# Output projections of token chunks 0-2 as products of 512 columns, the last 128 output columns computed transposed

## The chip, the cores and the metric

One core of a Trainium2 chip runs the whole kernel. The metric is the device time of one execution in microseconds (us). "Span" is the length of the profiled execution, about 2 us shorter than the time.

Engines: PE is TensorE, PEld its weight loads, DVE is VectorE, ACT is ScalarE; SPq and ACTq are the DMA issues on the SyncE and ScalarE queues. A "product" is one matmul instruction: PEld loads its stationary 128 x 128 operand (a weight load), and the columns of the other operand move past it. A "spread" is a DMA that copies 1/den to the partitions where DVE needs it; a "scaling" is the DVE pass that multiplies a part of phi(q) by it; the "scaled operand" PQ is what comes out.

## The reference, cut to what matters

```python
# x: 2048 tokens x 640; both branches read layernorm(x)
xn = _layernorm(x, axis=-1)
return x + _A_ref(xn, A_wqkv, A_wo) + _B_ref(xn, B_w1, B_b1, B_w2, B_b2)
# A: linear attention, 32 heads of 20, phi(q) (phi(k)^T v) / den, then @ wo
# B: gelu(xn @ w1 + b1) @ w2 + b2, 1536 hidden
```

The kernel folds attention's inner product and `wo` into a 640 x 640 matrix M. The output of a token is then 12 blocks of gelu(h) times W2 plus 5 blocks of the scaled phi(q) times M, plus x, plus b2: 17 products of 128 x 128 by 640 columns for each tile of 128 tokens. There are 16 tiles, in four chunks of four.

## The kernel before: the parts that matter

```python
# scaling phi(q) by 1/den, one chunk, on DVE: three passes, each behind its own "spread" DMA
def scale_pq(c): ...
    for r, (lo, n) in enumerate(((0, 2), (2, 2), (4, 1))):
        tensor_tensor(out=PQ[:, lo:lo+n, cc], in0=PQ[:, lo:lo+n, cc],
                      in1=rsp[:, c, r:r+1, :].broadcast_to(...), op=mult)
def spread(c): ...        # three DMAs on ACT's queue: rden -> rsp[:, c, r, :]
def x_again(c): ...       # reload of x, on the sync queue
# [... cut ...]
HALF = [(0, HW), (HW, D)]                 # HW = 320, D = 640: two PSUM banks a tile
out_mm(0, 0, JT, b0, HALF[:1], [b0])      # half of tile 0's first 12 products
den_mm(b0 + 1)                            # denominators
m_step(...)                               # M
den_rec()                                 # reciprocal on DVE
for c in range(NC): spread(c)
scale_pq(0)
# ... the first 12 products of tiles 3, 0, 1, 2 without the scaled operand ...
for t, b in enumerate(ahead):             # then their 5 products with it
    xb(t)                                 # x + b2 on DVE
    out_mm(t, JT, NS, b, HALF, [b, b + 1])
    out_done(t, b)                        # PSUM + (x + b2) on DVE, DMA out on the sync queue
for t in range(4, NT - 1):
    ...; out_mm(t, 0, NS, b, HALF, [b, b + 1]); out_done(t, b)
# [... last tile in three pieces ...]
```

Each of the 17 products of a tile is issued as two of 320 columns, with the same stationary operand loaded twice.

## Time and profile before

| | before |
|---|---|
| time, median of six runs | 207.47 us (207.40 to 207.63) |
| span | 205.6 us |
| products / weight loads recorded | 1539 / 1539 |
| PEld busy share | 66% |
| start of first output product to start of last DVE addition | 126.32 to 203.39: 77.07 us |

From the page of the kernel before: span, busy times and shares, then the chain of work that ended last, by engine.

```profile
span 205.6 us, 3863 instructions
...
PE 202.2 (98%) x1539; PEld 135.2 (66%) x1539; DVE 109.6 (53%) x227; ACT 71.4 (35%) x133; POOL 35.1 (17%) x85
...
PE 96%; DVE 1%; DMA 1%; issue 0%; ACT 0%; DVEq 0%
```

PE is the engine that bounds it. The timeline of PE in the kernel before (start, duration, engine, line, operation, operands, shape, count):

```profile
126.32 1.79 PE L671 MATMUL ps<-W,HG 128*128 128x320 bf16 x12
128.04 1.26 PE L618 MATMUL ps<-PQ,ZB 128*32 128x512 bf16 x20
129.13 1.80 PE L608 MATMUL ps<-Wo,W 128*32 128x320 bf16 x48
130.87 11.58 PE L671 MATMUL ps<-W,HG 128*128 128x320 bf16 x84
142.29 5.60 PE L671 MATMUL ps<-Msb,PQ 128*128 128x320 bf16 x40
...
152.34 3.42 PE L671 MATMUL ps<-W,HG 128*128 128x320 bf16 x24
...
156.96 3.42 PE L671 MATMUL ps<-W,HG 128*128 128x320 bf16 x24
```

Read starts, not durations: in this trace products overlap (24 of them have a duration of 3.42 us and a turn of 24 x 0.1358 = 3.26 us). A tile takes 156.96 - 152.34 = 4.62 us for 34 products, 135.8 ns each. The line at 142.29 is where PE first needs the scaled operand PQ; it follows without a gap.

The hand-over in the kernel before: the reload of x on the sync queue, the reciprocal, the twelve spreads, and the scalings of chunk 0 with what they waited for.

```profile
126.76 2.38 SPq L247 DMA_DIRECT2D xnT<-in_A_x_dram  x4
...
132.25 3.34 DVE L628 RECIPROCAL rden<-den_sb 128x512 bf16<-128x512 f32 x1
135.62 9.81 ACTq L247 DMA_DIRECT2D xn_tm<-rden  x12
138.83 0.69 DVE L633 TENSOR_TENSOR PQ<-PQ,xn_tm 128x1024 bf16<-128x1024 bf16 x1 [3.25 <-DMA xn_tm<-rden]
139.79 1.03 DVE L633 TENSOR_TENSOR PQ<-PQ,xn_tm 128x1024 bf16<-128x1024 bf16 x2 [0.27 <-DMA xn_tm<-rden]
```

The last scaling ends at 140.8. PE wants the first scaled block at 142.29, so there is room.

### The profile page before, as it was taken

To read this page: it belongs to the slowest core of one execution; us is meant where nothing else is said; L and a number is where in the kernel's file an instruction comes from. 1 tells how busy PE (TensorE), PEld (TensorE's weight loads), DVE (VectorE), ACT (ScalarE), POOL (GpSimd) and SP (SyncE) were. 2 spreads that over 40 slices of the span, in tenths; PEclk is the share of its full clock that TensorE was granted. 3 is DMA by queue.
4 is the path that set the end of the run, shared out by engine and by line. 5 is a ranking of instruction groups with operands and counts; after the bars stand their busy time and mean duration, and the time that the engine had idled before them with its cause. 6 is when DMAs were issued, how large, how long until landed. Compare 5 with 4: busy or idle time off the path is not lost.

```text
span 205.6 us, 3863 instructions
## 1 busy us (share of the span) xinstructions
PE 202.2 (98%) x1539; PEld 135.2 (66%) x1539; DVE 109.6 (53%) x227; ACT 71.4 (35%) x133; POOL 35.1 (17%) x85
## 2 busy tenths in 40 slices
PE   8999999999999999999999999999999999999995
PEld 3898767544457777777746445677777777777774
DVE  3784388100007888999358888734764322523322
ACT  2787777666676455111153554300000000000000
POOL 3342156800000001999000200000000000000000
PEclk9999999999999999999999999999999999999999
DMA  5967846699920000000000000968611100100111
GB/s 153 351 169 122 204 127 123 81 360 327 368 90 0 0 0 3 0 0 3 0 0 3 2 0 19 364 182 171 152 64 63 35 32 32 37 32 32 35 37 59
DMA packets 24842, 19.69 MB, mean 96 GB/s; under 512 B 9976, under 2 KB 24824, under 8 KB 24824
## 3 DMA queue, kind: packets, MB, share of 16 engines
q1 hardware_dynamic: 23072, 17.86, 29.5%
q10 hardware_dynamic: 1752, 1.58, 4.1%
q8 instruction: 12, 0.20, 0.4%
q14 instruction: 6, 0.05, 0.1%
HBM read 13.11 MB, written 2.62 MB: 77 GB/s over the span
## 4 chain that ended last, share of the span: by engine, by line
PE 96%; DVE 1%; DMA 1%; issue 0%; ACT 0%; DVEq 0%
PE ps L671 36%; PE ps L380 26%; PE ps L513 11%; PE ps L488 11%; PE ps L554 10%; DMA xPK<-in_A_x_dram 1%; DVE stats L331 1%; PE ps L608 1%; PE ps L564 1%; PE ps L618 1%; PE ps L318 0%; DVE xn_tm L353 0%; DVE W L722 0%; PE ps L361 0%; PE ps L537 0%
## 5 line engine op out<-in xcount | busy, mean ns | idle before, releaser
L671 PE MATMUL ps<-W,HG 128*128 128x320 bf16 (+2 forms) x396 | 54.8, 295 | 0.0
L380 PE MATMUL ps<-xnT,W 128*128 128x128 bf16 (+3 forms) x405 | 52.7, 292 | 0.1
L671 PEld LDWEIGHTS ps<-W,HG 128*128 128x128 bf16 x396 | 38.1, 98 | 14.5 <-ACT Msb L590 0.2
L380 PEld LDWEIGHTS ps<-xnT,W 128*128 128x128 bf16 x405 | 33.8, 98 | 18.4 <-DMA W<-in_B_w_dram 0.4
L384 ACT ACTIVATE HG<-ps,b1c 128x128 bf16<-128x128 f32 (+3 forms) x81 | 39.1, 515 | 14.4 <-PE ps L380 13.3
L682 DVE TENSOR_TENSOR W<-ps,xnT 128x640 bf16<-128x640 f32 x15 | 12.4, 825 | 35.8 <-PE ps L671 34.6
L476 ACT ACTIVATE ek<-ps 128x512 bf16<-128x512 f32 (+1 forms) x36 | 23.2, 645 | 20.4 <-PE ps L554 10.7
L477 DVE TENSOR_SCALAR ek<-ek 128x512 bf16<-128x512 bf16 (+1 forms) x36 | 11.0, 305 | 32.4 <-ACT ek L476 31.2
L671 PE MATMUL ps<-Msb,PQ 128*128 128x320 bf16 (+2 forms) x165 | 24.2, 295 | 0.0
L554 PE MATMUL ps<-xnT,Wqkv 128*128 128x512 bf16 x100 | 21.9, 379 | 0.0
L513 PE MATMUL ps<-xPK,xn_tm 128*128 128x320 bf16 x160 | 21.9, 299 | 0.0
L488 PE MATMUL ps<-Wqkv,xnT 128*128 128x320 bf16 x160 | 21.9, 299 | 0.0
L671 PEld LDWEIGHTS ps<-Msb,PQ 128*128 128x128 bf16 x165 | 15.9, 98 | 5.9
L488 PEld LDWEIGHTS ps<-Wqkv,xnT 128*128 128x128 bf16 x160 | 15.7, 98 | 6.2
L513 PEld LDWEIGHTS ps<-xPK,xn_tm 128*128 128x128 bf16 x160 | 15.7, 98 | 6.1
L507 POOL COPY Wqkv<-Wqkv 128x128 bf16<-128x128 bf16 x25 | 15.1, 603 | 22.9 <-PE ps L488 21.4
L331 DVE BATCH_NORM_STATS2 stats<-xPK 128x6 f32<-128x320 bf16 x32 | 14.0, 477 | 9.3 <-DMA xPK<-in_A_x_dram 9.2
L554 PEld LDWEIGHTS ps<-xnT,Wqkv 128*128 128x128 bf16 x100 | 9.7, 98 | 11.4
L479 DVE SCALAR_TENSOR_TENSOR PQ<-ps,ek 128x512 bf16<-128x512 f32 x20 | 13.8, 692 | 2.1
L479 DVE SCALAR_TENSOR_TENSOR xPK<-ps,ek 128x640 bf16<-128x640 f32 x16 | 13.2, 825 | 1.7
L525 DVE TENSOR_TENSOR Msb<-Msb,xPK 128x640 f32<-128x640 f32 x14 | 11.6, 825 | 0.5
L341 POOL TENSOR_TENSOR rstd<-aggr,mhalf 128x1 f32<-128x1 f32 x16 | 9.9, 620 | 8.9 <-DVE aggr L339 8.9
(57 smaller groups left out, 77.4 us busy)
## 6 DMA issues: line engine op xcount, KB each, us to landing
xnT<-in_A_x_dram SPq DMA_DIRECT2D x4, 640.0 KB, 6.8
Wqkv<-in_A_wqkv_dram SPq DMA_DIRECT2D x3, 800.0 KB, 6.8
out_dram<-W SPq DMA_DIRECT2D x15, 160.0 KB, 1.8
W<-in_B_w_dram SPq DMA_DIRECT2D x4, 480.0 KB, 6.1
W<-in_B_w_dram SPq DMA_DIRECT2D x1, 1920.0 KB, 13.0
xn_tm<-rden ACTq DMA_DIRECT2D x12, 128.0 KB, 3.4
xPK<-in_A_x_dram SPq DMA_DIRECT2D x4, 320.0 KB, 5.5
Wo<-in_A_wo_dram SPq DMA_DIRECT2D x8, 160.0 KB, 8.4
```

Of the source, the lines that this page charges most:

```text
L331: Pl.ins(v, lambda e: e.bn_stats(stats[:, s, 6 * h:6 * h + 6], x_in[:, t, h * HW:(h + 1) * HW]), reads=r_x[t], writes=[r_stats[s][h]])
L380: Pl.ins(pe, [(lambda e, k=k: e.matmul(bank(b, 0, w), W1[:, k, jb * P:(jb + 1) * P], xnT[:, k, tok], start=(k == 0), stop=(k == DT - 1))) ...
L384: Pl.ins(s_, lambda e: e.activation(HG[:, jb, tok], bank(b, 0, w), ACT.Gelu_apprx_tanh, bias=b1c[:, jb:jb + 1]), reads=[B_[b], r_b1c], wri ...
L476: Pl.ins(s_, lambda e: e.activation(e2, src, ACT.Exp), reads=br, writes=[r_ek[s]])
L479: Pl.ins(v, lambda e: e.scalar_tensor_tensor(out=d2, in0=src, scalar=0.0, in1=e2, op0=ALU.max, op1=ALU.add), reads=br + [r_ek[s]], writes= ...
L488: fns.append(lambda e, k=k, h=h, b=b, t=t: e.matmul(bank(b + h, 0, HW), xnT[:, k, t * P:(t + 1) * P], Wqkv[:, k, D + h * HW:D + (h + 1) * ...
L507: Pl.ins(g, lambda e, k=k, i=i: e.tensor_copy(plain(Wqkv[:, k, D:2 * D], i), parts(Wqkv[:, k, 0:D], i)), reads=[r_Wq], writes=[r_Wk, r_WqP])
L513: Pl.ins(pe, [(lambda e, t=t, h=h, b=b, f=f, i=i: e.matmul(bank(b + h, 0, HW), xn_tm[:, t, f * P:(f + 1) * P], PK[:, t, h * HW:(h + 1) * H ...
L525: Pl.ins(v, lambda e, t=t: e.tensor_tensor(out=zsum, in0=zsum, in1=PK[:, t, :], op=ALU.add), reads=[r_PK[t], r_zsum], writes=[r_zsum])
L554: Pl.ins(pe, [(lambda e, k=k, j=j, b=b: e.matmul(bank(b), Wqkv[:, k, D + j * P:D + (j + 1) * P], xnT[:, k, cc], start=(k == 0), stop=(k == ...
L671: Pl.ins(pe, [(lambda e, i=i, x=x, bb=bb: e.matmul(bank(bb, 0, x[1] - x[0]), seq[i][0], seq[i][1][:, x[0]:x[1]], start=(i == 0), stop=(i = ...
L682: Pl.ins(v, lambda e: e.tensor_tensor(out=halves(out_sb[:, s, :]), in0=pair(b), in1=halves(x_res[:, t, :]), op=ALU.add), reads=B_[b:b + 2] ...
```

## The change

Its intent is that all output products of chunks 0 to 2 have 512 columns, one full bank. Columns 0-511 go tile by tile: 17 products of 512 columns instead of 34 of 320. Columns 512-639 of a whole chunk are computed transposed: the 128 weight columns are stationary, the chunk's 512 tokens move, so another 17 products of 512. That result is transposed back by DMA before it is stored, and the matching part of x has to be transposed too before it can be added.

```diff
+        # x's last 128 columns: load in rows of 256 bytes, then transpose, on the sync queue
+        dma("sync", xrem..., xv[0:(NT - CH) * P, MW:D]..., [r_xrem] + r_PK)
+        for c in range(NC - 1):
+            dma_t("sync", xrT[:, c * CW:(c + 1) * CW]..., xrem[:, c * CW:(c + 1) * CW], [r_xrT[c]], reads=[r_xrem])
+        def rem_mm(c, lo, hi, b):       # stationary W2 / M columns 512-639, 512 tokens move
+        def rem_done(c, b):             # + b2 + xrT on DVE, dma_t back, DMA out (sync queue)
+        def main_done(t, b):            # 512 columns; DMA out now on ACT's queue
...
-        out_mm(0, 0, JT, b0, HALF[:1], [b0])
-        den_mm(b0 + 1)
+        out_mm(0, 0, JT, MAIN, first[:1])        # MAIN = [(0, 512)]
+        den_mm(bb[1])
...
-        for t, b in enumerate(ahead):
+        for t in range(1, CH):
+            out_mm(t, 0, JT, MAIN, first[t:t + 1])
+        rem_mm(0, 0, JT, first[CH])
+        for t in range(CH):
             xb(t)
-            out_mm(t, JT, NS, b, HALF, [b, b + 1])
-            out_done(t, b)
+            out_mm(t, JT, NS, MAIN, first[t:t + 1])
+            main_done(t, first[t])
...                                      # chunks 1, 2 alike; chunk 3 stays in halves
```

More of the change, by code (lines that the diff above doesn't have):

```diff
@@ L127, in bass_parallel_sum__linear_attn_block__dense_activation_gelu__prompt_kernel @@
     HH = H // 2
+    MW = D - P
     TA, TB = P // HH, P // H
@@ L183, in bass_parallel_sum__linear_attn_block__dense_activation_gelu__prompt_kernel @@
         out_sb = W1f[:, 2 * DT * D:2 * DT * D + 2 * D].rearrange("p (s d) -> p s d", s=2)
+        xPf = xPK[:].rearrange("p t d -> p (t d)")
+        xrT = xPf[:, 0:(NC - 1) * CW]
+        remT = xPf[:, (NC - 1) * CW:NC * CW]
+        remO = xPf[:, NC * CW:(NC + 1) * CW].rearrange("p (t d) -> p t d", t=CH)
+        xrem = xPf[:, (NC + 1) * CW:2 * NC * CW]
+        b2t = sb("b2t", [P, 1], BF16)
+        b2c = sb("b2c", [P, 1], FP32)
         ps = es.enter_context(nc.psum_tensor("ps", [P, 8 * 512], FP32))
@@ L234, in bass_parallel_sum__linear_attn_block__dense_activation_gelu__prompt_kernel @@
         r_out = [R_("out0"), R_("out1")]
+        r_xrT = [R_("xrT%d" % c) for c in range(NC - 1)]
+        r_xrem, r_remT, r_remO, r_b2t, r_b2c = R_("xrem"), R_("remT"), R_("remO"), R_("b2t"), R_("b2c")
         xv = A_x.rearrange("b s d -> (b s) d")
@@ L461, in bass_parallel_sum__linear_attn_block__dense_activation_gelu__prompt_kernel @@
             .rearrange("p a d -> p (a d)"), [r_b2])
+        dma("sync", b2t[:], B_b2[MW:D].rearrange("(p a) -> p a", a=1), [r_b2t])
         for w in range(NW):
@@ L646, in x_again @@
         def x_again(c):
-            dma("sync", x_res[:, c * CH:(c + 1) * CH, :],
-                xv[c * CW:(c + 1) * CW, :].rearrange("(t p) d -> p t d", p=P), [r_xr[c]] + (sum(r_xnT, []) if c == 0 else []))
+            w = MW if c < NC - 1 else D
+            dma("sync", x_res[:, c * CH:(c + 1) * CH, 0:w],
+                xv[c * CW:(c + 1) * CW, 0:w].rearrange("(t p) d -> p t d", p=P), [r_xr[c]] + (sum(r_xnT, []) if c == 0 else []))
         def xb(t):
-            Pl.ins(v, lambda e: e.tensor_tensor(out=x_res[:, t, :], in0=x_res[:, t, :], in1=b2bc[:], op=ALU.add),
+            w = MW if t < NT - CH else D
+            Pl.ins(v, lambda e: e.tensor_tensor(out=x_res[:, t, 0:w], in0=x_res[:, t, 0:w], in1=b2bc[:, 0:w], op=ALU.add),
                    reads=[r_xr[t // CH], r_b2], writes=[r_xb[t]])
@@ L661, in bass_parallel_sum__linear_attn_block__dense_activation_gelu__prompt_kernel @@
             x_again(c)
+        dma("sync", xrem.rearrange("p (t d) -> p t d", t=NT - CH),
+            xv[0:(NT - CH) * P, MW:D].rearrange("(t p) d -> p t d", p=P), [r_xrem] + r_PK)
+        for c in range(NC - 1):
+            dma_t("sync", xrT[:, c * CW:(c + 1) * CW].rearrange("p (t q) -> p t q", t=CH),
+                  xrem[:, c * CW:(c + 1) * CW], [r_xrT[c]], reads=[r_xrem])
+        Pl.ins(v, lambda e: e.tensor_copy(b2c[:], b2t[:]), reads=[r_b2t], writes=[r_b2c])
         b0 = take(2)
-        ahead = [(b0 + 2 * i) % 8 for i in range(4)]
@@ L665, in out_mm, with seq_of @@
-        def out_mm(t, lo, hi, b, w0, w1):
+        bb = [(b0 + i) % 8 for i in range(8)]
+        def seq_of(t):
             tok = slice(t * P, (t + 1) * P)
             seq = [(HG[:, jb, tok], W2[:, jb, :], [r_HG[t][jb], r_W2]) for jb in range(JT)]
-            seq += [(PQ[:, j, tok], Msb[:, j, :], [r_PQ[t // CH][j]] + r_M[j]) for j in range(DT)]
-            n = len(seq)
-            for i in range(lo, hi):
-                Pl.ins(pe, [(lambda e, i=i, x=x, bb=bb: e.matmul(
-                    bank(bb, 0, x[1] - x[0]), seq[i][0], seq[i][1][:, x[0]:x[1]],
-                    start=(i == 0), stop=(i == n - 1))) for x, bb in zip(w0, w1)],
-                    reads=seq[i][2], writes=[B_[bb] for bb in w1], mark=(i in (JT - 1, n - 1)))
+            return seq + [(PQ[:, j, tok], Msb[:, j, :], [r_PQ[t // CH][j]] + r_M[j]) for j in range(DT)]
@@ L676, in bass_parallel_sum__linear_attn_block__dense_activation_gelu__prompt_kernel, with out_mm @@
         NS = JT + DT
         HALF = [(0, HW), (HW, D)]
+        def out_mm(t, lo, hi, w0, w1):
+            seq = seq_of(t)
+            for i in range(lo, hi):
+                Pl.ins(pe, [(lambda e, i=i, x=x, bk=bk: e.matmul(
+                    bank(bk, 0, x[1] - x[0]), seq[i][0], seq[i][1][:, x[0]:x[1]],
+                    start=(i == 0), stop=(i == NS - 1))) for x, bk in zip(w0, w1)],
+                    reads=seq[i][2], writes=[B_[bk] for bk in w1], mark=(i in (JT - 1, NS - 1)))
+        def rem_mm(c, lo, hi, b):
+            cc = slice(c * CW, (c + 1) * CW)
+            seq = [(W2[:, jb, MW:D], HG[:, jb, cc], [r_HG[t][jb] for t in range(c * CH, c * CH + CH)] + [r_W2])
+                   for jb in range(JT)]
+            seq += [(Msb[:, j, MW:D], PQ[:, j, cc], [r_PQ[c][j]] + r_M[j]) for j in range(DT)]
+            for i in range(lo, hi):
+                Pl.ins(pe, lambda e, i=i: e.matmul(bank(b), seq[i][0], seq[i][1], start=(i == 0), stop=(i == NS - 1)),
+                       reads=seq[i][2], writes=[B_[b]], mark=(i in (JT - 1, NS - 1)))
@@ new lines, in rem_done @@
+        def rem_done(c, b):
+            cc = slice(c * CW, (c + 1) * CW)
+            Pl.ins(v, lambda e: e.scalar_tensor_tensor(out=remT, in0=bank(b), scalar=b2c[:, 0:1], in1=xrT[:, cc],
+                                                       op0=ALU.add, op1=ALU.add),
+                   reads=[B_[b], r_b2c, r_xrT[c]], writes=[r_remT])
+            dma_t("sync", remO, remT, [r_remO], reads=[r_remT])
+            dma("sync", ov[cc, MW:D].rearrange("(t p) d -> p t d", p=P), remO, [], reads=[r_remO])
@@ L679, in out_done @@
+        def main_done(t, b):
+            s = t % 2
+            Pl.ins(v, lambda e: e.tensor_tensor(out=out_sb[:, s, 0:MW], in0=bank(b), in1=x_res[:, t, 0:MW], op=ALU.add),
+                   reads=[B_[b], r_xb[t]], writes=[r_out[s]] + r_W1)
+            dma(s_, ov[t * P:(t + 1) * P, 0:MW], out_sb[:, s, 0:MW], [], reads=[r_out[s]])
         def out_done(t, b):
             s = t % 2
-            tok = slice(t * P, (t + 1) * P)
             Pl.ins(v, lambda e: e.tensor_tensor(out=halves(out_sb[:, s, :]), in0=pair(b),
@@ L684, in out_done @@
                    reads=B_[b:b + 2] + [r_xb[t]], writes=[r_out[s]] + r_W1)
-            dma("sync", ov[tok, :], out_sb[:, s, :], [], reads=[r_out[s]])
-        out_mm(0, 0, JT, b0, HALF[:1], [b0])
-        den_mm(b0 + 1)
-        m_step([0, 1, DT - 1, 2, 3], ahead[1:] + ahead[1:3], lambda: den_eps(b0 + 1))
+            dma("sync", ov[t * P:(t + 1) * P, :], out_sb[:, s, :], [], reads=[r_out[s]])
+        MAIN = [(0, MW)]
+        first = [bb[i] for i in (0, 6, 7, 1, 2)]
+        out_mm(0, 0, JT, MAIN, first[:1])
+        den_mm(bb[1])
+        m_step([0, 1, DT - 1, 2, 3], [bb[2], bb[4], bb[6], bb[2], bb[4]], lambda: den_eps(bb[1]))
         den_rec()
@@ L693, in bass_parallel_sum__linear_attn_block__dense_activation_gelu__prompt_kernel @@
         scale_pq(0)
-        out_mm(3, 0, JT, ahead[3], HALF[:1], [ahead[3]])
-        out_mm(0, 0, JT, b0, HALF[1:], [b0 + 1])
-        for t in range(1, 3):
-            b = ahead[t]
-            out_mm(t, 0, JT, b, HALF, [b, b + 1])
-        out_mm(3, 0, JT, ahead[3], HALF[1:], [ahead[3] + 1])
-        for t, b in enumerate(ahead):
+        for t in range(1, CH):
+            out_mm(t, 0, JT, MAIN, first[t:t + 1])
+        rem_mm(0, 0, JT, first[CH])
+        for t in range(CH):
             xb(t)
-            out_mm(t, JT, NS, b, HALF, [b, b + 1])
-            out_done(t, b)
+            out_mm(t, JT, NS, MAIN, first[t:t + 1])
+            main_done(t, first[t])
             if t == 1:
                 scale_pq(1)
-        for t in range(4, NT - 1):
-            b = ahead[t % 4]
+        rem_mm(0, JT, NS, first[CH])
+        rem_done(0, first[CH])
+        for c, bs in ((1, (3, 4, 5, 0, 6)), (2, (7, 1, 2, 3, 4))):
+            bs = [bb[i] for i in bs]
+            for t in range(c * CH, c * CH + CH):
+                b = bs[t % CH]
+                xb(t)
+                if t % CH == 2:
+                    scale_pq(c + 1)
+                out_mm(t, 0, NS, MAIN, [b])
+                main_done(t, b)
+            rem_mm(c, 0, NS, bs[CH])
+            rem_done(c, bs[CH])
+        for t, b in zip(range(NT - CH, NT - 1), (bb[6], bb[0], bb[2])):
             xb(t)
-            if t % CH == 2 and t // CH + 1 < NC:
-                scale_pq(t // CH + 1)
-            out_mm(t, 0, NS, b, HALF, [b, b + 1])
+            out_mm(t, 0, NS, HALF, [b, b + 1])
             out_done(t, b)
         t = NT - 1
-        ring[0] = ahead[t % 4]
+        ring[0] = bb[4]
         xb(t)
@@ L719, in bass_parallel_sum__linear_attn_block__dense_activation_gelu__prompt_kernel @@
             r_o = R_("ol%d" % i)
-            out_mm(t, 0, NS, b, [(lo, hi)], [b])
+            out_mm(t, 0, NS, [(lo, hi)], [b])
             s = t % 2
@@ L725, in bass_parallel_sum__linear_attn_block__dense_activation_gelu__prompt_kernel @@
             dma("sync", ov[tok, lo:hi], out_sb[:, s, lo:hi], [], reads=[r_o])
-        for ev in [ev for (waits, fns, ev, dma_) in Pl.records["sync"] if dma_][-4:]:
+        for ev in [ev for (waits, fns, ev, dma_) in Pl.records["sync"] if dma_][-7:]:
             Pl.wait_event("sync", ev)
```

## The prediction

> **What bounds the kernel now.** TensorE. The page shows PE busy 98% of a 205.6 us span at full clock; the chain of waits that ended last is 96% PE. The output stage runs on PE without a gap from 126.3 to 203.3 us (instructions in order of time); DVE mostly waits for PE there (34.6 us in the waits). Nothing before 126 us changes except one tiny load.
>
> **What changes on PE.** A token tile is now 34 products of 320 columns; tile starts lie 4.617 us apart (152.34, 156.96), so 135.8 ns each. The 40 products of 512 columns from 117.69 to 126.32 us take 215.8 ns each. Both fit 0.4167 ns a column plus about 2.5 ns a product, so the weight loads (98 ns each) are hidden in both forms. The Trainium skill ("TensorE: Matmul & The Clock Gate", section "Wait — 56ns, not 53.3ns?") names the same: N / 2.4 GHz plus about 2.5 ns; this trace agrees. A chunk before: 4 x 34 x 135.8 = 18.47 us. After: 4 x 17 + 17 = 85 products x 215.8 = 18.34 us. The columns streamed are the same; only 51 fixed costs a chunk vanish. Three chunks: 153 x 2.5 ns, about 0.39 us, all on the critical path. The 153 weight loads saved (15 us of PEld busy) were hidden and are worth nothing.
>
> **What it adds and moves.** Off PE: three transposes of x by DMA, three of the output, 256-byte row loads and stores, one DVE pass a chunk (about 0.7 us, as 128x512 from PSUM takes now), less in the per-tile passes (640 to 512 columns). DVE is some 40% busy in this stage, so this hides. The banks rotate over all eight; each was drained several tiles earlier. Tiles 12-15 and the tail are unchanged.
>
> **Where it can cost.** The hand-over, 128-143 us. The half-tile before the denominators becomes a whole one (12 products, +0.96 us), so reciprocal and spreading DMAs start 0.96 us later: reciprocal ends at about 136.6, the first scaling at 140.5, the third at 141.8. PE gets to the scaled operand at 131.8 + 48 x 0.2158 = 142.2. The slack is 1.3-1.7 us. In this stretch DMA was 97%, 91%, 65%, 85% busy (four-us windows from 128 us); now the small-row load of x (1536 rows of 256 B) and three transposes (2.6 us to landing for 128x640 before) run against the spreads (3.2-4.4 us to landing). The skill ("DMA: Bandwidth & Descriptors", section "Specifications") asks 512 B for full rate, so these rows cost more than their bytes; no such transfer in this stretch shows it yet. If the chunk-0 spreads take over 5 us, PE waits: a wait of 0.3-1.5 us has one chance in three, expected +0.15 us. The first output DMAs, now behind twelve spreads on ACT's queue, delay DVE by 2-3 us, but no bank that PE needs.
>
> **Prediction.** 207.47 - 0.39 + 0.15: 207.2 us; range 206.8 to 208.5. Faster by over 2%: 0.01; within 2%: 0.97; slower by over 2%: 0.02.
>
> **What would show it.** Right: output products at 215.8 ns; 153 fewer products and weight loads; PE's output stage shorter by about 0.4 us; no PE wait on banks; DVE still waiting for PE; same tail. Wrong: a PE gap before the first products on PQ (near 142 us), with spreads landing after over 5 us.
>
> **What would make it wrong.** DMA contention stalling PE beyond 2 us; weight loads not hidden before, which would make the gain larger; a bank drained late because DVE sits on an output slot or a transposed x.

## The result, and the profile after

| | before | after |
|---|---|---|
| time, median of six runs | 207.47 us (207.40 to 207.63) | 207.54 us (207.16 to 207.98) |
| products / weight loads recorded | 1539 / 1539 | 1375 / 1386 (11 product records missing) |
| PEld busy share | 66% | 59% |
| first output product to last DVE addition | 77.07 us | 76.69 us (this profile) |

The ratio is 1.0004, 95% interval 0.9985 to 1.0023: the same time. Ratios here are the mean of one kernel's fast runs over the mean of the other's of the same rounds, so not quite the ratio of the medians quoted. The six runs after are 207.16, 207.16, 207.17 and 207.91, 207.94, 207.98: two groups, where before had one. The profile comes from a run of 207.16 us.

The page after, the same lines:

```profile
span 205.1 us, 3575 instructions
...
PE 200.5 (98%) x1375; PEld 120.1 (59%) x1386; DVE 109.4 (53%) x231; ACT 71.3 (35%) x133; POOL 35.2 (17%) x85
...
PE 95%; DVE 1%; DMA 1%; ACT 1%; issue 1%; DVEq 0%
```

PE's timeline after:

```profile
126.18 2.75 PE L696 MATMUL ps<-W,HG 128*128 128x512 bf16 x12
128.87 1.26 PE L630 MATMUL ps<-PQ,ZB 128*32 128x512 bf16 x20
129.96 1.80 PE L620 MATMUL ps<-Wo,W 128*32 128x320 bf16 x48
131.92 7.72 PE L696 MATMUL ps<-W,HG 128*128 128x512 bf16 x35 [0.16 <-ACT Msb L602]
139.47 2.75 PE L707 MATMUL ps<-HG,W 128*128 128x512 bf16 x12
142.06 4.48 PE L696 MATMUL ps<-Msb,PQ 128*128 128x512 bf16 x19
...
147.46 2.75 PE L696 MATMUL ps<-W,HG 128*128 128x512 bf16 x12
...
165.80 2.75 PE L696 MATMUL ps<-W,HG 128*128 128x512 bf16 x12
```

Chunk 1 takes 165.80 - 147.46 = 18.34 us for 85 products, 215.8 ns each. Before, four tiles took 4 x 4.617 = 18.47 us. The gain that was forecast is there, product by product: 77.07 - 76.69 = 0.38 us for the stage. The 0.16 us before 131.92 is as before: there PEld waited 0.2 us for the same copy of M by ACT.

The hand-over after (this view ends at 146 us, so it counts 10 of the twelve spreads):

```profile
129.21 0.41 SPq L258 DMA_DIRECT2D xPK<-in_A_x_dram  x1
...
133.07 3.34 DVE L640 RECIPROCAL rden<-den_sb 128x512 bf16<-128x512 f32 x1
136.44 9.70 ACTq L258 DMA_DIRECT2D xn_tm<-rden  x10
138.54 6.13 SPq L261 DMA_TRANSPOSE xPK<-xPK  x3
...
139.64 0.69 DVE L645 TENSOR_TENSOR PQ<-PQ,xn_tm 128x1024 bf16<-128x1024 bf16 x1 [3.23 <-DMA xn_tm<-rden]
140.79 1.13 DVE L645 TENSOR_TENSOR PQ<-PQ,xn_tm 128x1024 bf16<-128x1024 bf16 x2 [0.45 <-DMA xn_tm<-rden]
```

The last scaling ends at 141.9. PE reaches the fifth block of PQ, which the third scaling delivers, at 142.06 + 4 x 0.216 = 142.9. One microsecond is left; before, it was 142.29 + 8 x 0.136 - 140.8 = 2.6 us. The transposes of x are issued in the middle of the spreads.

Share of the DMA engines by window, kernel before (columns: window, its length, busy of PE, PEld, DVE, ACT, POOL, clock, DMA share, GB/s):

```profile
136.00:140.00 4.00, 4.00 (x32) 2.86 (x31) 0.90 (x2) 0.00 (x0) 0.00 (x0) 1.00 0.65 123
140.00:144.00 4.00, 4.00 (x32) 2.90 (x30) 1.37 (x4) 0.00 (x0) 0.00 (x0) 1.00 0.85 172
```

And after:

```profile
136.00:140.00 4.00, 4.00 (x20) 1.85 (x19) 0.77 (x2) 0.00 (x0) 0.00 (x0) 1.00 0.54 97
140.00:144.00 4.00, 3.95 (x19) 1.77 (x19) 2.45 (x6) 0.00 (x0) 0.00 (x0) 1.00 1.06 181
```

From 140 us the DMA engines are full (I read 1.06 as no more than that) at nearly the same GB/s (181 and 172).

So the trace of a short run shows the whole gain, and the median shows none of it. The question is what the other runs lose.

### The profile page after: what moved, and what is told of

Read it like the earlier page. It is cut to its first block, busy times and chain, and to the rows that moved or that the text cites. A ratio compares the mean times of both kernels' runs of the same rounds, so it can differ in the third digit from the quotient of the medians.

```text
span 205.1 us, 3575 instructions
## 1 busy us (share of the span) xinstructions
PE 200.5 (98%) x1375; PEld 120.1 (59%) x1386; DVE 109.4 (53%) x231; ACT 71.3 (35%) x133; POOL 35.2 (17%) x85
## 4 chain that ended last, share of the span: by engine, by line
PE 95%; DVE 1%; DMA 1%; ACT 1%; issue 1%; DVEq 0%
PE ps L696 30%; PE ps L391 25%; PE ps L525 11%; PE ps L500 11%; PE ps L566 10%; PE ps L707 5%; DMA xPK<-in_A_x_dram 1%; DVE stats L342 1%; ACT Msb L602 1%; PE ps L576 1%; PE ps L630 1%; PE ps L329 0%; DVE xn_tm L364 0%; DVE W L775 0%; PE ps L372 0%
## 5 line engine op out<-in xcount | busy, mean ns | idle before, releaser
L696 PE MATMUL ps<-W,HG 128*128 128x512 bf16 (+3 forms) x249 | 46.4, 338 | 0.3 <-ACT Msb L602 0.2
L696 PEld LDWEIGHTS ps<-W,HG 128*128 128x128 bf16 x252 | 24.0, 98 | 20.4 <-ACT Msb L602 0.2
L566 PE MATMUL ps<-xnT,Wqkv 128*128 128x512 bf16 x97 | 21.4, 379 | 0.2
L696 PE MATMUL ps<-Msb,PQ 128*128 128x512 bf16 (+3 forms) x104 | 20.8, 338 | 0.1
L720 DVE TENSOR_TENSOR W<-ps,xnT 128x512 bf16<-128x512 f32 x12 | 8.3, 691 | 18.2 <-PE ps L696 12.6
L696 PEld LDWEIGHTS ps<-Msb,PQ 128*128 128x128 bf16 x105 | 10.1, 98 | 8.4
```

Source lines behind the costliest of these rows:

```text
L566: Pl.ins(pe, [(lambda e, k=k, j=j, b=b: e.matmul(bank(b), Wqkv[:, k, D + j * P:D + (j + 1) * P], xnT[:, k, cc], start=(k == 0), stop=(k == ...
L696: Pl.ins(pe, [(lambda e, i=i, x=x, bk=bk: e.matmul(bank(bk, 0, x[1] - x[0]), seq[i][0], seq[i][1][:, x[0]:x[1]], start=(i == 0), stop=(i = ...
```

## The experiments

Theory A: in some runs the hand-over loses what was gained or more (0.8 us was expected before the runs), because the transposes and the load of small rows compete with the spreads. Rival B: the two groups come from elsewhere, such as the start of the kernel or DVE's wait for output slots. Later A was split: A1, the transposes do it; A2, the small-row load does it; A3, it also takes the slack that the whole first tile used up.

All "stage" numbers are from the start of the first output product to the start of the last DVE addition in that run's profile.

### The changed kernel again (three times)

No edit.

> The changed kernel again, unaltered. The six runs of it so far fall in two groups, 207.16-207.17 (three) and 207.91-207.98 (three), 0.78 us apart; the kernel before shows no such split (207.40-207.63). Theory A (the gain of 0.39 us is there in every run, and in some runs the hand-over at 128-143 us loses about 0.8 us to contention of the small-row load and the transposes with the spreads): the split appears again, on one chip, within one series; if the profile falls on a long run, it shows a PE gap near 142 us. Rival B (the groups are two chips, or the start of the kernel): all runs on this one chip fall in one group, or the gap lies before 126 us.

> The changed kernel unaltered, for another profile. Theory: the time from first output product to last addition is 76.69 us plus the PE gap before the scaled operand and nothing else; the gap is smaller the later the transposes start after the spreads (2.10 us after: no gap; 1.43: 0.48; 0.05: 0.97). Rival: some profile shows a longer stage with no gap there.

> As the one before, one look. Theory and rival as there. Runs near 207.2 us should belong to a profile without the gap, runs of 207.6 us and more to one with it.

Measured: 207.57 us median of six runs (207.14 to 207.76; ratio 1.0008, 0.9995 to 1.0020), 207.71 us of four (207.47 to 208.06; 1.0014, 0.9999 to 1.0029), and one run of 207.86 us. The three profiles have stages of 77.17, 77.14 and 77.19 us, that is 0.48, 0.45 and 0.50 us over the 76.69 of the first profile. Two neat groups did not come back; the values spread. On these chips the kernel before spreads as well (207.03 to 207.84), and the first output product starts anywhere from 126.12 to 126.57 us over all profiles, so the start of the kernel blurs the total by about as much as the effect under study. Rival B is right about that part. It is wrong about the rest: a loss of 0.45 to 0.50 us lies inside the output stage, though not the 0.8 us that theory A expected. The run of 207.86 us, as long as the long group of the first series, has both, a late start (126.42 us) and the gap; no trace of the three long runs of that series is at hand. The single look, in order of time (again cut at 146 us):

```profile
136.68 9.62 ACTq L258 DMA_DIRECT2D xn_tm<-rden  x10
137.88 6.13 SPq L261 DMA_TRANSPOSE xPK<-xPK  x3
...
139.91 0.69 DVE L645 TENSOR_TENSOR PQ<-PQ,xn_tm 128x1024 bf16<-128x1024 bf16 x1 [3.26 <-DMA xn_tm<-rden]
141.59 0.69 DVE L645 TENSOR_TENSOR PQ<-PQ,xn_tm 128x1024 bf16<-128x1024 bf16 x1 [0.99 <-DMA xn_tm<-rden]
142.29 1.03 PE L696 MATMUL ps<-Msb,PQ 128*128 128x512 bf16 x3
143.17 0.43 DVE L645 TENSOR_TENSOR PQ<-PQ,xn_tm 128x512 bf16<-128x512 bf16 x1 [0.89 <-DMA xn_tm<-rden]
...
143.66 2.55 PE L696 MATMUL ps<-Msb,PQ 128*128 128x512 bf16 x11 [0.33 <-DVE PQ L645]
```

The first scaling is on time. The second and the third wait 0.99 and 0.89 us for their spreads, and PE stops before the fifth block until the third scaling ends at 143.6. (One of the four products before the gap is not recorded; 143.66 - 142.29 less four products of 0.216 us is a loss of 0.51 us. The 0.33 us in brackets is less because the profile counts a product as busy longer than its turn.) In the profile without a gap the transposes began 2.10 us after the spreads; in the three with one, 1.43, 1.37 and 1.20 us after (stages 77.17, 77.14 and 77.19 us, so among these three the order is not strict).

### The load of small rows and its transposes early

```diff
+        # xrem load and its three dma_t, moved here
         for c in range(NC):
             x_again(c)
-        # xrem load and its three dma_t
```

> The load of the last 128 columns of x and its three transposes are issued ahead of the reload of x, so they run at about 104-115 us, where the DMA engines stand idle, instead of at 128-144 us. PE's order is unchanged. Theory A (contention at the hand-over causes the long group): every run near 207.1 us, no long group. Rival B (something else causes it, such as the start or the longer ACT queue): the same two groups, 207.16 and 207.95. Spreads should land in 3.2-3.5 us instead of 4.2 in either case.

> The early load again, unaltered, as the candidate that beats both kernels: by theory 153 fixed costs, -0.39 us against the kernel before, ratio 0.9981; the earlier five runs gave 0.9991 with an interval that just held 1. Rival (no gain beyond noise): ratio 1.000.

Measured: 207.17 us (206.97 to 207.38; ratio 0.9991, 0.9979 to 1.0003) and again 207.17 us (207.13 to 207.41; 0.9988, 0.9976 to 1.0000). Stage 76.69 us in both profiles, no gap, scalings waiting 3.3 and 0.2 us. The transposes ran from about 106.5 us. This shows that load and transposes together cause the loss, not yet which of the two.

### The early load, and the output DMAs back on the sync queue

```diff
-            dma(s_, ov[t * P:(t + 1) * P, 0:MW], out_sb[:, s, 0:MW], ...)
+            dma("sync", ov[t * P:(t + 1) * P, 0:MW], out_sb[:, s, 0:MW], ...)
```

> As the early load, and the twelve output DMAs of the tiles go on the sync queue again instead of ACT's, where they wait for the twelve spreads to be issued. The 5.3 us wait of DVE for an output slot at 147-152 us should shrink to about 1 us. Theory: DVE is not on the critical path, so no change against the early load alone beyond 0.1 us (207.1 us). Rival: the backlog of DVE is what costs time in the long group; then this one alone has no long runs while the early load still has them.

Measured: 207.28 us (207.02 to 207.33; 0.9994, 0.9982 to 1.0006), stage 76.68 us. DVE's longest wait for an output slot is 5.3 us after the change, 2.0 us with the early load and 1.1 us here; the stage does not answer to it. The DVE backlog is off the critical path.

### The fixed cost of a product, by itself

The kernel before, with products 1 to 15 of the 17 of tiles 4 to 14 cut once more.

```diff
+                cut = quarters and 0 < i < n - 1     # 2 x 160 columns instead of 320
```

A first form that cut all 17 opened a second accumulation in a bank while the first was still open. The first and last product therefore stay whole.

> The kernel before, with the products 1-15 of the 17 of tiles 4-14 cut once more, 320 columns into 2 x 160: 330 products and weight loads more, the same columns. Theory (a product costs its columns at 0.4167 ns plus about 2.5 ns, weight loads hidden even at 160 columns): 330 x 2.5 ns = +0.83 us, 208.3 us. Rival (a weight load of 98 ns binds as soon as a product takes less, 69 ns here): 330 x 2 products at 98 ns instead of 69, about +19 us more. Second rival (the fixed cost is not real, the gain of the change came from elsewhere): +0, 207.5 us.

Measured: 208.21 us (208.06 to 208.42; ratio 1.0042, 1.0030 to 1.0054), stage 77.89 us: 0.82 us more than before for 330 products, 2.5 ns each. PE's timeline there:

```profile
147.62 3.48 PE L674 MATMUL ps<-W,HG 128*128 128x320 bf16 x46
...
152.31 3.48 PE L674 MATMUL ps<-W,HG 128*128 128x320 bf16 x46
```

A tile takes 4.69 us where it took 4.62. Every weight load is still recorded at 98 ns, PEld is 72% busy over the span and 97% from 150 to 160 us, and a 160-column product takes only 69 ns of PE (160 x 0.4167 + 2.5); the loads stay hidden. That they fit is because their records overlap: 138 loads of 98 ns stand in those 10 us. Both rivals fall. What no run separates: every product added here, or removed by the change, brought or took its own weight load, so the 2.5 ns could belong to the product or to the change of weights.

### Only the transposes of x removed

```diff
-        for c in range(NC - 1):
-            dma_t("sync", xrT..., xrem..., [r_xrT[c]], reads=[r_xrem])
...
-                                                       in1=xrT[:, cc],
+                                                       in1=xrem[:, cc],
```

> The changed kernel without the three transposes of x; the small-row load stays where it is. Wrong on purpose: the untransposed x is added. Theory A1 (the transposes delay the second and third spread of chunk 0; the load of small rows is done by then and does not): no PE gap before the first products on PQ, first output product to last DVE addition 76.68 us as with the early load, scaling waits 3.3 and 0.2 us. Rival A2 (the small-row load does it, by its packets): the gap of the repeated run (0.48 us) is there in some profiles, second and third scaling late.

Measured: a wrong result; 207.26 us (206.93 to 207.60; 0.9987, 0.9975 to 1.0000), stage 76.68 us, no gap, scalings waiting 3.2 and 0.3 us. The small-row load was still there, issued at 129.40 and landed 8.6 us later, and did no harm to the spreads issued from 136.63:

```profile
139.82 0.69 DVE L645 TENSOR_TENSOR PQ<-PQ,xn_tm 128x1024 bf16<-128x1024 bf16 x1 [3.23 <-DMA xn_tm<-rden]
140.77 1.03 DVE L645 TENSOR_TENSOR PQ<-PQ,xn_tm 128x1024 bf16<-128x1024 bf16 x2 [0.26 <-DMA xn_tm<-rden]
...
142.25 4.48 PE L693 MATMUL ps<-Msb,PQ 128*128 128x512 bf16 x19
```

A2 falls.

### Load early, transposes at the moment of the spreads

```diff
+        # xrem load moved ahead of x_again, as in the early load; its three dma_t removed there
...
         for c in range(NC):
             spread(c)
+        for c in range(NC - 1):
+            dma_t("sync", xrT..., xrem..., [r_xrT[c]], reads=[r_xrem, r_rden])
```

> The small-row load early, in idle time, but the three transposes of x held until the reciprocal is done, so that they are issued at the same moment as the spreads (about 136.5 us) instead of 1.4-2.1 us after it. Theory A1 (transposes against spreads): the suspected cost in full, without the load: all three scalings of chunk 0 late, a PE gap near 142 us in every run, 0.5 to 2.5 us; 207.7 to 209.5 us. Rival A2 (the load did it): no gap, 76.7 us for the stage, 207.2 us.

Measured: 208.01 us (207.76 to 208.41; ratio 1.0028, 1.0017 to 1.0040), stage 77.66 us, 0.97 us over 76.69. The hand-over:

```profile
136.75 9.39 ACTq L258 DMA_DIRECT2D xn_tm<-rden  x10
136.80 5.46 SPq L261 DMA_TRANSPOSE xPK<-xPK  x3
...
142.37 0.59 PE L693 MATMUL ps<-Msb,PQ 128*128 128x512 bf16 x2
142.62 0.69 DVE L645 TENSOR_TENSOR PQ<-PQ,xn_tm 128x1024 bf16<-128x1024 bf16 x1 [1.40 <-DMA xn_tm<-rden]
143.59 0.38 PE L693 MATMUL ps<-Msb,PQ 128*128 128x512 bf16 x1 [0.63 <-DVE PQ L645]
```

With the transposes beside the spreads from the first moment, PE now waits for the second scaling and then for the third. The load was out of the way here, so the transposes alone do it, and in these profiles a later start after the spreads went with a smaller loss: 0.05 us after, 0.97 us lost; 1.2 to 1.4 after, 0.45 to 0.50; 2.10 after, nothing (one profile).

### Transposes of x after chunk 0's spreads have landed

```diff
-        # the three dma_t behind the xrem load
...
+            dma_t("sync", xrT..., xrem..., [r_xrT[c]], reads=[r_xrem] + r_rsp[0])   # behind spread()
```

> The changed kernel with the transposes of x held until the three spreads of chunk 0 have landed (about 141 us); the load stays where it is. Theory A1: no gap at the scaled operand, 76.7 us from first output product to last addition, total as the early load (207.1-207.2 us). Rival A2 (the load): gap as in the repeated run in some runs. A second possible cost: the later transposes hold up the first addition of the last 128 columns (needs its x at about 147 us), and with it DVE, but no bank that PE needs soon.

Measured: 207.31 us (207.16 to 207.60; 0.9992, 0.9979 to 1.0005), stage 76.68 us, no gap. Transposes began at 141.60. DVE waited up to 3.7 us for an output slot, which PE did not notice. The second possible cost did not appear.

### Six of tile 0's twelve first products moved behind M

```diff
-        out_mm(0, 0, JT, MAIN, first[:1])
+        out_mm(0, 0, JT // 2, MAIN, first[:1])
         den_mm(bb[1]); m_step(...); ...; scale_pq(0)
+        out_mm(0, JT // 2, JT, MAIN, first[:1])
```

> The changed kernel, but only 6 of the 12 first products of tile 0 stand before the denominators, the other 6 after the product steps for M. The same products; the reciprocal and the spreads start 6 x 0.2158 = 1.3 us earlier, PE gets to the scaled operand at the same time. Theory A3 (the wait needs two things, the transposes of x beside the spreads and the short slack left by the whole first tile): no PE gap in any profile, 76.7 us from first output product to last addition, total 207.1-207.2 us in a series without long runs, though load and transposes stay where the change put them. Rival (slack does not matter because the earlier spreads meet the end of the small-row load and land later by as much): the gap stays.

> The same 6 products moved, on the kernel whose transposes are issued at the moment of the spreads, where a gap of 0.97 us stood in the profile (77.66 us for the stage, 208.0 us). Theory A3: 1.3 us more slack covers a lateness of 0.97 us: 76.7 us, 207.2 us, and the scalings still wait long for their spreads (about 3.8, 1.4, 0.4 us). Rival (the gap follows the transposes whatever the slack): 77.5 us or more.

Measured: with the change's own load and transposes, 207.01 us (206.91 to 207.29; ratio 0.9984, 0.9970 to 0.9997), stage 76.68 us, no gap. With the transposes held to the moment of the spreads, 207.22 us (206.87 to 207.65; 0.9990, 0.9973 to 1.0007), stage 76.68 us: the 0.97 us is gone although the scalings there still wait 3.9, 1.1 and 0.7 us. From the profile of the first of the two:

```profile
135.16 11.60 ACTq L258 DMA_DIRECT2D xn_tm<-rden  x12
138.72 6.51 SPq L261 DMA_TRANSPOSE xPK<-xPK  x3
139.13 1.63 DVE L645 TENSOR_TENSOR PQ<-PQ,xn_tm 128x1024 bf16<-128x1024 bf16 x3 [4.00 <-DMA xn_tm<-rden]
...
142.08 4.26 PE L696 MATMUL ps<-Msb,PQ 128*128 128x512 bf16 x19
```

And from the second:

```profile
142.27 4.48 PE L693 MATMUL ps<-Msb,PQ 128*128 128x512 bf16 x20
142.44 0.43 DVE L645 TENSOR_TENSOR PQ<-PQ,xn_tm 128x512 bf16<-128x512 bf16 x1 [0.74 <-DMA xn_tm<-rden]
```

In the first, the spreads start 1.3 us earlier than after the change, their first one takes 0.8 us longer to come (the wait is 4.0 instead of 3.2 us), so the rival has a point; but all three scalings end by 140.8, and PE needs the third at 142.9. By itself this run does not test the slack: its transposes began 3.6 us after the spreads, later than the 2.10 us of the profile that had no gap anyway. The second does, as its transposes began 0.06 us after the spreads: the third scaling is late, it ends at 142.87, and PE needs it at 142.27 + 4 x 0.216 = 143.13. A3 holds by it: the gap needs both the transposes and the short slack. The first of these two is also the only correct version whose interval against the kernel before lies wholly below 1, with a mean 0.16% lower; as one of twelve comparisons with 95% intervals, that is a weak sign, and the evidence for the gain is the stage. In the same series the unaltered change had 207.71 us.

## Why the prediction was right, and where a size was off

- **The range.** 207.2 us in 206.8 to 208.5 was predicted, 207.54 us measured; the same within 2%, as forecast. That is a weak test: the range holds the result with the gap and without it, and "the same" would have held for any change under 4 us. The terms below test the reasoning.
- **The gain, 153 x 2.5 ns = 0.39 us.** Shown: 0.38 us in the stage without a gap, chunk 1 in 18.34 us as worked out, and 2.5 ns again from the 330 products added by themselves. The Trainium skill ("TensorE: Matmul & The Clock Gate", section "Wait — 56ns, not 53.3ns?") states this cost and the traces here agree (215.8, 135.8 and 69 ns for 512, 320 and 160 columns).
- **The hidden weight loads are worth nothing.** Shown: 153 loads fewer with the change, 330 more with the cut products, and in both cases the stage moves by 2.5 ns a product with its load (which of the two it belongs to is not shown here).
- **The term that was mis-sized: "a wait of 0.3-1.5 us has one chance in three, expected +0.15 us".** The wait is where the text put it, and its size of 0.45 to 0.50 us lies in the stated range, but three of the four profiles of the unaltered change have it. Three quarters of 0.48 is 0.36 us, an estimate from four profiles; 207.47 - 0.39 + 0.36 = 207.44, against 207.54 measured. So the gain is given back at the hand-over in most runs.
- **The cause inside that term.** The text blamed "the small-row load of x" together with the transposes. The runs clear the load at the moment where the change puts it: with it in place and the transposes gone there is no gap, and with it gone and the transposes at the spreads the gap is largest. The load matters only indirectly, as the transposes wait for it: it landed 9.3 us after its issue in the profile without a gap and 8.4 to 8.6 us in the three with one. It is not cleared for earlier spreads: with half a tile moved, the first spread took 3.9 us instead of 3.2 before any transpose had begun, with the load still under way (landed at 138.7). No run separates that load from the reload of x there.
- **The sign "If the chunk-0 spreads take over 5 us, PE waits"** was right. Of chunk 0's three spreads the slowest landed 3.7 us after its issue in the profile without a gap, 5.1 us in each of the three with one, 5.4 us with the transposes at the moment of the spreads, and 3.4 us with the early load or without transposes. The slowest of all twelve says little: 5.5 us without a gap, 5.7 to 5.8 with one. The 5 us hold for the slack of the change: with half a tile moved and the transposes at the spreads, 5.5 us made no gap.
- **The slack, 1.3-1.7 us,** was worked out for undisturbed spreads and holds for those: with the early load the third scaling ends at 141.5 and is needed at 142.9.
- **DVE's backlog behind ACT's queue,** put at 2-3 us, is one wait of 5.3 us, but off the path, as said: cutting it to 1.1 us changed nothing.

What stays open: why the small-row load lands sooner in some executions than in others, and whether the transposes delay the spreads at the issue of descriptors or in the DMA engines. Both queues' issue times grow (twelve spreads took 9.2 us to issue with the early load and 11.1 us in the single look above; three transposes 6.1 us instead of 3.8), and the engines are full as well; no run here separates the two. In the single look the engines moved 119 GB/s from 140 to 142 us at a share of 1.13; with the early load it was 169 GB/s at 0.82. The spread of the totals beyond the gap was traced only as far as the varying start of the first output product.

## What to carry to other kernels

Here PE was busy without gaps and the weight loads were hidden, and making products wider saved only the fixed cost of each product removed (2.5 ns); in such a case count the products and multiply before building anything. A change that streams the same columns with fewer instructions can be paid for at the one point where PE depends on a chain through other engines: look there at what the new DMAs run beside and at how much slack the reordering has used. Put a DMA transpose where the queues are idle, or move independent PE work behind the start of the chain; and when the total varies at its start, compare a stage of the traces, which here repeats to 0.01 us when PE does not wait.

## What the Trainium skill lacked or had wrong

- "DMA: Bandwidth & Descriptors", section "Rules for kernel authors", says that a transpose next to ordinary DMAs needs nothing. That is said of correctness, and the results here agree; what the pairing costs in time is missing. The second scaling could start 4.1 us after the issue of the spreads began when no transpose ran (second profile of the early load), 4.9 us after it in the single look at the changed kernel, and 5.9 us after it with the transposes issued at the same moment; three transposes took 5.5 to 6.5 us to issue beside the spreads and 3.8 us alone.
- "Perfetto Trace Analysis", section "Identifying the Most-Contended Engine", proposes the busy share of the weight loads, beside MFU (the arithmetic done as a share of the peak), as a measure of how near PE is to its limit. That share is 59%, 66% and 72% of the span for the same multiplications, and 45%, 72% and 97% inside the output stage (from 150 to 180, 190 and 160 us), while the stage moves from 76.69 to 77.07 and 77.89 us, just 2.5 ns for each product. Summed load by load, as the page does it, the last would be 138 x 98 ns in 10 us, 135%. In these kernels the share measures how finely the work is cut, not the room left.
- "DMA: Bandwidth & Descriptors", section "Specifications", asks for 512 bytes or more for full rate. The load in rows of 256 bytes (384 KB) landed in 3.4 to 3.6 us when issued early, in idle time, and in 8.4 to 9.5 us behind the reload of x. No run compares it with longer rows of the same volume, so the rule is neither confirmed nor refuted here.
